# A new program order for the attention stage and the first weight conversions, with the engine of each PSUM copy chosen anew

## The chip, the cores and the metric

The kernel runs on one core of a Trainium2 chip as one program. The metric is the device time of that program in microseconds (us). The median of three runs of the kernel before is 977.77 us (975.89 to 978.73). The profile is one further execution: it took 975.42 us, of which the trace covers a span of 973.6 us.

A core has five engines, each with its own instruction queue that runs strictly in order: TensorE (PE for its matmuls, PEld for its weight loads), VectorE (DVE), ScalarE (ACT), GpSimd (POOL) and SyncE (SP), which here issues nearly all DMAs. They wait for one another by semaphores only. TensorE writes to PSUM, and what it writes has to be copied out by VectorE or ScalarE.

## What is computed

Three layers follow one another:

```python
# 4 x 8 heads, 576 positions, 64 dimensions: rotary attention
q_rot, k_rot = rotate(q), rotate(k)
scores = matmul(q_rot, k_rot.T) / sqrt(D)
attn = exp(scores - max(scores)); attn /= sum(attn) + 1e-9
x = matmul(attn, v)                      # 2304 tokens x 512
# dense layer, 512 -> 2048 -> 512
h = maximum(x @ w_in, 0); x = (h * h) @ w_out
# one of 8 experts per token, 512 -> 1024 -> 512, scaled by the gate
out[mask] = gate[mask] * (maximum(x[mask] @ w1[e], 0) @ w2[e])
```

## The kernel before, in words

Attention is cut into 16 problems, numbered p = 0 to 15, each of two heads. The work on one problem is a set of named steps. These are the names that the texts use:

- `ldq`, `ldk`, `ldv` load q, k, v by DMA; there is one buffer each for raw q and raw k. `aq bq cq` and `ak bk ck` are the rotary products and their sum (128x576 each, lines 189 to 194).
- `qh`, `kh` round q and k to the fast matmul type (line 198). `ql`, `kl0`, `kl1` take the rest that rounding left (lines 205, 208). `qd0` to `qd2` and `kd0` to `kd2` move halves between partitions (line 212), by DMA or by an engine.
- `sc0` to `sc8` are nine score tiles (line 233): four matmuls of 288 columns each, ten for `sc8`. They go into **two** PSUM buffers in turn. `mx` takes the row maximum of a score tile on VectorE (line 248), `ex` the exponential with its row sum on ScalarE (line 258). Only when `ex` has read a score buffer may TensorE write into it again, so a score tile waits for the exponential of the tile two places earlier in TensorE's order.
- `trm..`, `trrk`, `trrq`, `trrr` transpose the exponentials on TensorE (line 291): four matmuls each, one for `trrr`. `evm..`, `evrk`, `evrq`, `evrr`, `sev` copy the results out of PSUM (lines 308, 274). `pv0`, `pv1` multiply by v, 20 matmuls each (line 323), and `u0`, `u1` copy that out. Transposes and products share four PSUM buffers.
- `sa`, `srec` prepare the reciprocal of the row sums, `rst` stores them. `xr` stores the result; for the first 512 tokens `rld`, `xn`, `xh`, `xl`, `xst` divide and split it at once.

The dense layer needs its weights rounded to the reference's type and split in two parts. Weight piece i goes through `wd` (DMA), `wx` (two ScalarE instructions, lines 474 and 475), `wy` (two on VectorE, lines 479 and 480), `wz` (GpSimd, line 484), `wb` (VectorE, line 490), `wh` (ScalarE, line 504) and `wl` (VectorE or GpSimd, line 507). Two pieces make one of 16 weight chunks. The pieces 0 to 11, up to `wb10`, `wh9` and `wl9`, are steps of the written order; the rest is converted inside the loop of the dense layer, `Weights.slot`. `m10`, `m11`, `m12` are the first-layer matmuls of chunks 0 to 2 of the first 512 tokens, with `re`, `sq` (ScalarE) and `gg`, `gl` (VectorE) after each; `m20` is the second-layer product of chunk 0, which reads `sq0` and `gl0`.

The order is written out by hand. A table gives each step a number and an engine (`D` SP's DMA queue, `T` TensorE, `V` VectorE, `A` ScalarE, `P` GpSimd): `FIRST` for problem 0, `SECOND` for 1, `THIRD` for 2 and 3, `PLAN` for 4 to 15, `TAIL` for the weights and the start of the dense layer. The number plus 18 times p is a sorting key, no more. Line 403 sorts all steps by it and emits them, so the key sets the place in the queue of the step's engine; the semaphores set the time.

```python
        plan = [(t + p * PERIOD, p, name, eng) for p in range(NP)
                for name, (t, eng) in (FIRST, SECOND, THIRD, THIRD, PLAN)[min(p, 4)].items()
...
        for t, p, name, eng in sorted(plan, key=lambda z: z[0]):
```

Of the kernel before, what the change touches and what calls it, by code (L numbers as in the profile page):

```python
# [21 lines left out]
B, H, S, D = 4, 8, 576, 64  # L22
# [12 lines left out]
def f32(ap):  # L35
# [23 lines left out]
}  # L59
FIRST = {  # L60
# [20 lines left out]
}  # L81
SECOND = {
# [19 lines left out]
}  # L102
THIRD = {
# [1129 lines left out]
```

## Time and profile before

| what | value |
|---|---|
| median of three runs | 977.77 us |
| profiled execution, and its span | 975.42 us, 973.6 us |
| TensorE busy, VectorE busy | 908.2 us (93%), 615.4 us (63%) |
| ScalarE busy, GpSimd busy | 468.8 us (48%), 323.1 us (33%) |
| first score matmul | 20.23 us |
| first matmul of the dense layer | 326.43 us |

The time divides at 326.43 us: attention ahead of it, with weight conversions in between, and behind it the dense layer and the experts. Matmuls are pipelined and the end of each is modelled, so the busy time of TensorE counts latencies too: gaps between its weight loads say more. From about 410 us on TensorE's matmuls stand without gaps up to about 900 us.

### The profile page before, as it was taken

To read this page: it belongs to the slowest core of one execution; us is meant where nothing else is said; L and a number is where in the kernel's file an instruction comes from. 1 tells how busy PE (TensorE), PEld (TensorE's weight loads), DVE (VectorE), ACT (ScalarE), POOL (GpSimd) and SP (SyncE) were. 2 spreads that over 40 slices of the span, in tenths; PEclk is the share of its full clock that TensorE was granted. 3 is DMA by queue.
4 is the path that set the end of the run, shared out by engine and by line. 5 is a ranking of instruction groups with operands and counts; after the bars stand their busy time and mean duration, and the time that the engine had idled before them with its cause. 6 is when DMAs were issued, how large, how long until landed. Compare 5 with 4: busy or idle time off the path is not lost. (4 is left out here: it accounts for less than half of the span.)

```text
span 973.6 us, 14639 instructions
## 1 busy us (share of the span) xinstructions
PE 908.2 (93%) x5210; PEld 748.4 (77%) x5210; DVE 615.4 (63%) x1120; ACT 468.8 (48%) x946; POOL 323.1 (33%) x258
## 2 busy tenths in 40 slices
PE   1889899989989999999999999999999999999996
PEld 0767667767767676788888888888988889999995
DVE  5776666776766799947554654665373856666650
ACT  3666666666666777542223223222333345555551
POOL 6776775675673366601001100100010123112011
PEclk9999999999999999999999999999999999999998
DMA  7566556546644556451003001100141268777630
GB/s 244 154 177 186 151 132 167 154 119 170 200 122 128 172 169 204 127 165 53 1 1 120 11 1 60 28 1 1 44 173 66 87 182 263 233 223 242 203 107 34
DMA packets 51233, 123.48 MB, mean 127 GB/s; under 512 B 11072, under 2 KB 15184, under 8 KB 51152
## 3 DMA queue, kind: packets, MB, share of 16 engines
q1 hardware_dynamic: 48112, 112.76, 38.6%
q0 software_dynamic: 3040, 9.70, 2.8%
q8 instruction: 43, 0.70, 0.3%
q14 instruction: 38, 0.31, 0.1%
HBM read 93.45 MB, written 15.54 MB: 112 GB/s over the span
## 5 line engine op out<-in xcount | busy, mean ns | idle before, releaser
L250 DVE TENSOR_REDUCE nmx<-sc 128x1 f32<-128x576 f32 x144 | 106.8, 750 | 81.1 <-PE sc L245 80.9
L650 PE MATMUL h<-xs,w 128*128 128x512 f32 (+1 forms) x660 | 145.6, 369 | 4.8 <-DVE w L507 4.6
L656 ACT ACTIVATE r<-h 128x512 f32<-128x512 f32 (+1 forms) x80 | 44.2, 553 | 215.1 <-PE h L650 202.6
L245 PE MATMUL sc<-kh,q 128*128 128x288 f32 (+2 forms) x336 | 102.8, 340 | 46.1 <-ACT e L261 25.2
L261 ACT ACTIVATE e<-sc,nmx 128x576 f32<-128x576 f32 x144 | 106.3, 741 | 76.4 <-DVE nmx L250 76.0
L650 PEld LDWEIGHTS h<-xs,w 128*128 128x128 f32 x660 | 115.1, 188 | 30.0 <-DVE w L507 7.6
L664 DVE SCALAR_TENSOR_TENSOR h<-h,r 128x512 f32<-128x512 f32 (+1 forms) x80 | 51.5, 644 | 124.5 <-ACT r L656 124.3
L684 PE MATMUL y<-w,gh 128*128 128x512 f32 x396 | 122.7, 391 | 0.0
L245 PEld LDWEIGHTS sc<-kh,q 128*128 128x128 f32 x336 | 62.9, 196 | 74.3 <-ACT e L261 44.9
L922 DVE TENSOR_TENSOR w<-eraw,w 128x1024 fp32r<-128x1024 f32 x64 | 78.4, 1226 | 33.5 <-ACT w L921 33.4
L245 PE MATMUL sc<-kl,q 128*128 128x288 f32 (+2 forms) x336 | 91.5, 306 | 0.0
L303 PE MATMUL b<-ident,e 128*128 128x128 f32 x640 | 86.0, 274 | 2.4 <-ACT e L261 2.0
L684 PEld LDWEIGHTS y<-w,gh 128*128 128x128 f32 x396 | 73.3, 188 | 14.5
L571 POOL TENSOR_TENSOR xraw<-xraw,rbs 128x512 f32<-128x512 f32 (+1 forms) x14 | 16.6, 1191 | 197.0 <-DMA rbs<-rD 193.5
L684 PE MATMUL y<-w,gl 128*128 128x512 f32 x198 | 77.1, 389 | 0.0
L968 PEld LDWEIGHTS h<-ye,w 128*128 128x128 f32 x576 | 74.0, 189 | 3.7
L303 PEld LDWEIGHTS b<-ident,e 128*128 128x128 f32 x640 | 73.6, 141 | 3.8 <-ACT e L261 2.9
L968 PE MATMUL h<-ye,w 128*128 128x256 f32 x576 | 74.8, 280 | 0.0
L991 PE MATMUL y<-w,ge 128*128 128x512 f32 x288 | 74.6, 394 | 0.0
L332 PE MATMUL b<-et,v 128*64 128x288 f32 x512 | 73.0, 425 | 0.1
L921 ACT ACTIVATE w<-eraw 128x1024 fp32r<-128x1024 f32 x64 | 67.3, 1052 | 4.1 <-DMA eraw<-wexp 4.1
L998 POOL DMA_INDIRECT out<-ob,six x19 | 22.2, 1169 | 140.1 <-ACT ob L997 107.8
(213 smaller groups left out, 1701.4 us busy)
## 6 DMA issues: line engine op xcount, KB each, us to landing
eraw<-wexp SPq DMA_DIRECT2D x64, 512.0 KB
wraw<-wio SPq DMA_DIRECT2D x32, 512.0 KB
rawq<-qx SPq DMA_DIRECT2D x15, 576.0 KB
rawk<-kx SPq DMA_DIRECT2D x15, 576.0 KB
kh<-kh SPq DMA_DIRECT2D x45, 144.0 KB
v<-v SPq DMA_DIRECT2D x16, 320.0 KB
q<-ql SPq DMA_DIRECT2D x32, 144.0 KB
yD<-ysb SPq DMA_DIRECT2D x18, 256.0 KB
```

What stands on the lines that cost most here:

```text
L245: nc.tensor.matmul(out=o[:, x:x + w], lhsT=q[:, hd, q0:q0 + 128], rhs=k[:, hd, y:y + w], start=(n == 0), stop=(n == len(ops) - 1))
L250: nc.vector.tensor_reduce(out=m, in_=sc(p, j)[:, :, 0:HS], axis=AX.XY, op=ALU.max, negate=True)
L261: nc.scalar.activation(out=e(p)[:, o:o + S].rearrange("p (a b) -> p a b", a=2), in_=sc(p, j)[:, :, 0:HS], func=ACTF.Exp, bias=live[p, f"nm ...
L303: nc.tensor.transpose(t[:, i * 128:(i + 1) * 128], x[:, o:o + 128], ident)
L332: nc.tensor.matmul(out=o[64 * hd:64 * hd + 64], lhsT=lhsT, rhs=rhs, start=(c == 0), stop=(c == 4))
L650: nc.tensor.matmul(out=h, lhsT=w[:, a, k * 128:(k + 1) * 128], rhs=xs[b, k][:, c], start=(k == 0 and i == 0), stop=(k == 3 and i == 2))
L664: nc.vector.scalar_tensor_tensor(out=h, in0=h, scalar=W_SC, in1=rs[n], op0=ALU.mult, op1=ALU.mult)
L684: nc.tensor.matmul(out=yp[t], lhsT=g[a][:, t * 128:(t + 1) * 128], rhs=w[:, c, 512:1024], start=(f == 0 and i == 0), stop=(f == NFC - 1 an ...
L921: nc.scalar.activation(out=w[:, 0], in_=r, func=ACTF.Copy)
L922: nc.vector.tensor_tensor(out=w[:, 1], in0=r, in1=f32(w[:, 0]), op=ALU.subtract)
L968: nc.tensor.matmul(out=h, lhsT=w[:, a, k * 128:(k + 1) * 128], rhs=x[:, c], start=(k == 0 and i == 0), stop=(k == 3 and i == 2))
L991: nc.tensor.matmul(out=yp[s, t], lhsT=g[a][:, t * 128:(t + 1) * 128], rhs=w[:, c, 512:1024], start=(f == 0 and i == 0), stop=(f == EFC - 1 ...
```

## The change

Only the numbers and engine letters of the five tables change. No step is added or removed, and no function changes; two lines of `PLAN` and one of `TAIL` stand here for all.

```diff
-    "ak": (-98.423, "P"), "ck": (-97.690, "P"), "kh": (-97.204, "A"), "cq": (-96.360, "P"), "qh": (-94.409, "V"),
-    "kd0": (-94.211, "D"), "ql": (-93.978, "V"), "kd1": (-93.003, "D"), "kl0": (-92.725, "P"), "qd0": (-92.656, "D"),
...
+    "qh": (-102.8623, "A"), "ql": (-102.7975, "P"), "ldk": (-101.9928, "D"), "ak": (-100.9528, "P"),
...
-    "wx4": (-254.209, "A"), "wy3": (-251.056, "V"), "wb2": (-215.057, "V"), "wz3": (-210.181, "P"),
...
+    "wx4": (-286.6154, "A"), "wy4": (-275.3811, "V"),
```

In `PLAN`, `qh` goes from VectorE to ScalarE, `ql` from VectorE to GpSimd, and `kl1` from GpSimd to VectorE; of the copies, `evm02`, `evm03`, `evm11`, `evrq`, `evrr` and `u1` go from ScalarE to VectorE and `evm00`, `evm01`, `evm12`, `evrk` and `u0` the other way; `evm10`, `sev` and `evm13` stay. In `FIRST` all three `qd` and `kd` moves are made by engines and none by DMA, and k is rotated ahead of q. Of the loaded pieces of the weights, 6 to 10 are converted earlier.

On TensorE, in the written order of problems 9 and 10, this stood between the end of one score tile (`sc2`, here sc_2194) and the start of the one that takes its PSUM buffer (`sc4`, here sc_2223); sc_2208 is `sc0`, and the row with ident is one transpose step of four matmuls.

```order
L245 MATMUL sc_2194<-kl0_87,q0_83 128x288
L303 MATMUL b_2203<-ident_63,e1_90 128x128 x4
L245 MATMUL sc_2208<-kh0_85,q0_83 128x288
L245 MATMUL sc_2208<-kl0_87,q0_83 128x288
L245 MATMUL sc_2208<-kh0_85,q0_83 128x288
L245 MATMUL sc_2208<-kl0_87,q0_83 128x288
L245 MATMUL sc_2223<-kh0_85,q0_83 128x288
```

In the changed kernel the same three tiles are sc_2193, sc_2234 and sc_2251, and this stands between them on TensorE (L303 is `trrr`).

```order
L254 MATMUL sc_2193<-kl0_87,q0_83 128x288
L312 MATMUL b_2201<-ident_63,e1_90 128x128 x4
L312 MATMUL b_2208<-ident_63,e1_90 128x128 x4
L312 MATMUL b_2213<-ident_63,e1_90 128x128 x4
L312 MATMUL b_2218<-ident_63,e1_90 128x128 x4
L254 MATMUL sc_2234<-kh0_85,q0_83 128x288
L254 MATMUL sc_2234<-kl0_87,q0_83 128x288
L254 MATMUL sc_2234<-kh0_85,q0_83 128x288
L254 MATMUL sc_2234<-kl0_87,q0_83 128x288
L303 MATMUL b_2241<-ident_63,e1_90 128x128
L254 MATMUL sc_2251<-kh0_85,q0_83 128x288
```

Three more transpose steps and `trrr` have moved in between the two tiles that share a buffer; the pair of tiles after them was spread in the same way.

On ScalarE, in the same place, these rows stood from the exponential of `sc1` (sc_2163) to that of `sc2` (sc_2194): the row sums `rs`, two pieces of `rk` and one copy `et1`.

```order
L261 ACTIVATE e0_89<-sc_2163,nmx_2183 128x576
L176 ACTIVATE rs_2199<-b_2185 9x128
L176 ACTIVATE rk1_92<-b_2185 64x64 x2
L176 ACTIVATE et1_2170<-b_2188 128x512
L261 ACTIVATE e0_89<-sc_2194,nmx_2215 128x576
```

In the changed kernel (problems 11 and 12 here, whose rows are alike) the two exponentials stand next to each other, with copies ahead of them and behind them.

```order
L185 ACTIVATE et0_2555<-b_2600 128x512
L270 ACTIVATE e0_89<-sc_2583,nmx_2612 128x576
L270 ACTIVATE e0_89<-sc_2606,nmx_2637 128x576
L185 ACTIVATE et1_2576<-b_2621 128x512
L185 ACTIVATE et1_2576<-b_2626 128x512
```

The copies that stood between the two exponentials are gone from there. At the start of the dense layer VectorE had these rows from `gg0` (h_3491) to `gg1`, with weight conversions (L479 to L507) between them.

```order
L664 SCALAR_TENSOR_TENSOR h_3491<-h_3491,r_3517 128x512
L668 TENSOR_TENSOR gl_3522<-h_3491,gh_3519 128x512
L507 TENSOR_TENSOR wf_3478<-wmag_3458,wf_3478 128x512
L490 SCALAR_TENSOR_TENSOR wmag_3480<-wraw_3256,wmag_3480 128x512
L664 SCALAR_TENSOR_TENSOR h_3504<-h_3504,r_3542 128x512
```

In the changed kernel chunk 1 comes first (h_3510), then chunk 0 (h_3534, whose `gl0` is gl_3579) and chunk 2 (h_3559).

```order
L673 SCALAR_TENSOR_TENSOR h_3510<-h_3510,r_3523 128x512
L488 TENSOR_SCALAR wmag_3528<-wmag_3528 128x512
L489 TENSOR_SCALAR wmag_3528<-wmag_3528 128x512
L677 TENSOR_TENSOR gl_3554<-h_3510,gh_3552 128x512
L673 SCALAR_TENSOR_TENSOR h_3534<-h_3534,r_3557 128x512
L516 TENSOR_TENSOR we_3459<-wmag_3292,we_3459 128x512
L673 SCALAR_TENSOR_TENSOR h_3559<-h_3559,r_3574 128x512
L677 TENSOR_TENSOR gl_3579<-h_3534,gh_3572 128x512
L677 TENSOR_TENSOR gl_3584<-h_3559,gh_3582 128x512
```

`gl0` now stands behind `gg2`, which waits for the matmuls of chunk 2, and fewer conversions stand among these rows.

## Rows read from the trace of the kernel before

**Rows 1.** The page: the span.

```profile
span 973.6 us, 14639 instructions
```

**Rows 2.** Stretches: us, then busy per engine (instructions), granted clock, DMA share, GB/s.

```profile
20.20:96.84 76.64, 65.90 (x444) 52.51 (x444) 52.86 (x73) 47.76 (x117) 56.23 (x43) 0.98 0.63 176
96.84:318.68 221.84, 204.23 (x1474) 155.39 (x1473) 152.37 (x225) 142.29 (x356) 139.33 (x109) 0.98 0.54 150
209.89:228.02 18.13, 16.78 (x125) 12.86 (x124) 12.38 (x19) 11.57 (x30) 11.40 (x9) 1.00 0.55 156
340.00:405.00 65.00, 60.41 (x256) 47.02 (x255) 62.95 (x94) 46.25 (x81) 44.03 (x31) 1.00 0.56 181
```

**Rows 3.** Waits, 96.8 to 318.7 us: total us, times, longest.

```profile
PEld sc L245 <- ACT e L261: 32.3, 67, 1.6
```

**Rows 4.** Waits, 20.2 to 96.8 us.

```profile
PEld sc L245 <- ACT e L261: 12.6, 15, 2.0
```

**Rows 5.** Timeline, weight loads of one problem: start, us, what, [idle before, releaser].

```profile
211.72 0.19 PEld L245 LDWEIGHTS sc<-kh,q 128*128 128x128 f32 x1 [0.15 <-ACT e L261]
...
212.27 0.45 PEld L303 LDWEIGHTS b<-ident,e 128*128 128x128 f32 x4
...
212.99 0.19 PEld L245 LDWEIGHTS sc<-kh,q 128*128 128x128 f32 x1 [0.27 <-ACT e L261]
...
215.10 0.19 PEld L245 LDWEIGHTS sc<-kh,q 128*128 128x128 f32 x1 [1.55 <-ACT e L261]
...
215.82 0.19 PEld L245 LDWEIGHTS sc<-kh,q 128*128 128x128 f32 x1 [0.16 <-ACT e L261]
...
216.54 1.65 PEld L332 LDWEIGHTS b<-et,v 128*64 128x64 f32 x16 [0.16 <-issue]
...
219.12 0.19 PEld L245 LDWEIGHTS sc<-kh,q 128*128 128x128 f32 x1 [0.44 <-issue]
```

**Rows 6.** Timeline, VectorE and ScalarE in the same problem.

```profile
210.05 0.75 DVE L250 TENSOR_REDUCE nmx<-sc 128x1 f32<-128x576 f32 x1
...
210.84 0.74 ACT L261 ACTIVATE e<-sc,nmx 128x576 f32<-128x576 f32 x1 [0.54 <-DVE nmx L250]
...
212.56 0.76 DVE L250 TENSOR_REDUCE nmx<-sc 128x1 f32<-128x576 f32 x1 [0.42 <-PE sc L245]
...
213.73 0.60 ACT L176 ACTIVATE et<-b 128x512 f32<-128x512 f32 x1
...
214.22 0.73 ACT L261 ACTIVATE e<-sc,nmx 128x576 f32<-128x576 f32 x1
```

**Rows 7.** Groups by line and shape: busy us, mean ns, idle before.

```profile
L178 DVE CAST q<-rawq 128x576 fp32r<-128x576 f32 x15 | 24.3, 1620 | 10.6 <-POOL rawq L194 10.6
...
L176 ACT ACTIVATE q<-rawq 128x576 fp32r<-128x576 f32 x1 | 0.7, 666 | 0.0
```

**Rows 8.** Line 181 on VectorE: ns min/median/max, first and last start.

```profile
L181 DVE TENSOR_TENSOR ql<-rawq,q x16: 748/758/1965, 13.2 to 291.5; 128x576 fp32r<-128x576 f32 x16
```

**Rows 9.** Timeline, the preparation of k and q: issues of SP, work of GpSimd.

```profile
199.32 1.11 SPq L220 DMA_DIRECT2D kh<-kh  x1
...
201.45 1.42 POOL L181 TENSOR_TENSOR kl<-rawk,kh 64x576 fp32r<-64x576 f32 x1 [0.96 <-DMA kh<-kh]
...
201.66 0.33 SPq L187 DMA_DIRECT2D rawq<-qx  x1
...
206.21 1.43 POOL L192 TENSOR_TENSOR rawq<-rawq,tabq 128x576 f32<-128x576 f32 x1 [3.35 <-DMA rawq<-qx]
```

**Rows 10.** Timeline, the start: ScalarE's first weight piece and the first score matmul.

```profile
11.95 0.64 ACT L475 ACTIVATE wraw<-wraw 128x512 f32<-128x512 uint32 x1
...
20.23 0.58 PE L245 MATMUL sc<-kh,q 128*128 128x288 f32 x1 [20.23 <-ACT kh L176]
```

**Rows 11.** Waits, 326 to 410 us.

```profile
PEld h L650 <- DVE w L507: 7.6, 8, 1.0
```

203 rows, old and new, of tables (FIRST, PLAN, SECOND, TAIL) are left out of this document.

## The prediction

> **What bounds the kernel now.** I read the stretches first [rows 2]. TensorE is the engine with the most busy time in attention, 16.78 of 18.13 us for one problem, against 12.38 on VectorE, 11.57 on ScalarE and 11.40 on GpSimd. From 340 to 405 us it is VectorE, 62.95 of 65. So in attention the question is what TensorE waits for. The list of waits has one answer: the exponentials on ScalarE, which free the score buffers, 32.3 us in 67 waits from problem 4 on and 12.6 us in the first four [rows 3, 4]. The timeline of one problem shows where [rows 5]: 0.15, 0.27, 1.55 and 0.16 us ahead of four score tiles, 2.13 us in all. The gaps of 0.16 and 0.44 around the product with v wait for no other engine ("issue"). I count them as TensorE's own; some of the 32.3 us are such gaps under another name.
>
> Why is one wait 1.55 us? Rows 6 show a tile that is served at once and one that isn't. Served at once: maximum from 210.05, exponential from 210.84, weight load of the next tile at 211.72 [rows 5, 6], so 1.67 us from the start of the maximum. A maximum starts 0.29 us after the tile's last issue (212.27 to 212.56). A score buffer is therefore away for at least 1.96 us, and TensorE needs that much other work between two tiles of one buffer. Ahead of `sc4` it has one score tile (211.72 to 212.27, 0.55) and one transpose step (0.45), 1.0 us. Besides, ScalarE makes a 0.60 us copy at 213.73 and smaller ones before it, while the maximum has been ready since 213.32: the exponential starts at 214.22, 0.9 us late.
>
> **The change, part by part.** It removes and adds no instruction; it moves them.
>
> *Problems 4 to 15.* In the new order I add up, with the same prices, TensorE's work between two tiles of one buffer. One score tile is 0.55, one transpose step 0.45, `sc8` 10/4 of a score tile or 1.4, a product with v with its gaps 2.6 (216.54 to 219.12). Ahead of `sc3` of the next problem stand `sc8` and two steps, 2.3; of `sc1` two steps, one tile, two steps, 2.35; of `sc2` the same; of `sc0` six steps and a tile, 3.25; of `sc4` four steps, a tile and `trrr`, 2.4 at least; of `sc6`, `sc5`, `sc7` and `sc8` a product and a tile, 3.15 each. None is under 1.96. Then the engines have to serve at once. On ScalarE a single copy (`evm01`, 0.60) may stand ahead of `ex1`, and `sc0`, which waits for that, has 3.25; `ex2` follows directly. `qh` stands ahead of `ex8`: there the maximum of the long `sc8` isn't ready any earlier. VectorE has at most one large copy, of about that size, between two maxima. So the 2.13 us per problem should go but for a few hundredths: I take 2.1 x 12 = 25.2 us. What is late next is TensorE itself, at 18.13 - 2.13 = 16.0 us per problem. Bounds: 0, if the waits only move, and 32.3, all of rows 3.
>
> What must stay hidden for this: `qh` costs VectorE 1.62 and ScalarE 0.67 [rows 7]. ScalarE with 11.57 of 18.13 has room for it and VectorE is relieved. `ql` on GpSimd, at the price of the other GpSimd pieces (1.42), replaces `kl1` there, so its 11.40 per problem stay and fit into 16.0. The earlier weight pieces stand in the gaps that VectorE keeps between `sc4` and `sc6`, where TensorE makes 2.6 us of product; without that cover each would cost about such a copy, 0.6 us, once.
>
> *Problems 0 to 3.* The same rule, but rotation is shared with VectorE and the interleaving is different in each, and `pv0` and `pv1` come one problem later, which leaves TensorE something to do while it waits. I take half of the waits on exponentials, 6 us. Bounds: 3 lost to 12.6 gained [rows 4].
>
> *The start.* ScalarE's first weight piece ends at 12.59, the first score is at 20.23 [rows 10]. In the new order k is rotated first, and behind that weight piece ScalarE has `kh`, `kd0`, `kd1`, `qh`, `qd0`, two instructions of a weight piece, `kd2`, `qd1`: nine at about 0.66 [rows 7, 10], 5.9 us, to 18.5. That is 1.7 us gained; bounds 0 and 2.5. DMAs no longer make q's moves there, so `ldq` of problem 1 is freed earlier, too.
>
> *The dense layer.* TensorE waits eight times 0.95 us for converted weights, while VectorE is full [rows 2, 11]. With fewer conversions left behind attention VectorE comes in ahead, and the lead is used up over the ten chunks: I take half, 3.8 us. On the other side `gl0` now stands behind `gg2`. `m20` reads `gl0` after two matmuls, and nothing but it is queued on TensorE: from the end of `m12` it waits for `re2`, `gg2` and `gl0`, three instructions of 128x512. At the 0.60 of such a copy [rows 6] I estimate 1.8 us lost. Together 2.0 gained; bounds 1.8 lost and 7.6 gained.
>
> *Sum.* 25.2 + 6 + 1.7 + 2.0 = 34.9 us off the profiled execution of 975.42 (span 973.6 [rows 1], 1.8 around it): 940.5. The median of the runs stands 2.35 above that execution, so 943 us.
>
> **A rule that speaks against it.** VectorE's two-input subtraction takes 0.758 us in the median and up to 1.965 [rows 8]; `kl1` is now one of these, beside GpSimd's rotation. The Trainium skill, in "SBUF — State Buffer", section "Who interferes with whom", says that a VectorE instruction with two SBUF inputs shares a port pair with a GpSimd instruction that reads SBUF, and whichever comes second waits for all of the other. By it `kl1` would take 0.76 and up to 1.4 more in each problem and push the next maximum by some 0.3 us; the sum would be 12 x 0.3 = 4 us higher, 947. The median of rows 8 doesn't show it, the maximum may.
>
> **The rivals.**
> 1. *The waits move only in part.* Copies are shared out anew, and the product with v needs the last of them; if half of the 2.13 us comes back there or at a maximum, the problems give 12.8 instead of 25.2, the first four 3: 19.5 off, 958 us. For it: both engines stand within a few tenths of being late for `sc3` and `sc4`. Against: rows 5 show each wait with a cause that the new order takes away.
> 2. *Attention becomes faster than I say.* All of rows 3 and 4 that isn't "issue" goes and the weight waits vanish: 27 + 12.6 + 1.7 + 5.8 = 47 off, 931 us. For it: nothing in the sums above forbids it. Against: the first problems also wait for their own k and q.
> 3. *Slower: the single buffer of raw k becomes the loop.* `ldk` now waits for `kl1`, which stands on VectorE behind the last maxima. A load of 576 KB takes 4.55 us from issue to the first use (201.66 to 206.21 [rows 9]); then `ql`, `ak`, `bk`, `ck` on GpSimd, 4 x 1.42 = 5.7; `kh` 0.7; the move 2.1 (199.32 to 201.45); `kl1` 0.8: 13.9 us, under 16.0. With waits for a place in each queue it decides from 2.1 us more on. At 16.0 all is as forecast; to eat up the other 9.7 us of gain too it has to reach 18.13 + 0.8 = 18.9. At 19.5 the kernel takes 12 x 1.37 = 16.4 more and 9.7 less: 984 us. For it: GpSimd waits 3.35 us for such a load already, and it is in order, so `sa` and `kl0` are queued behind. Against: 2.1 us of room, and the DMA share of 0.55 is far from full.
> 4. *It doesn't do what it says:* the loop is held at 18.1 by something that no view shows, and only start and dense layer count: 3.7 off plus 0 to 6, 971 us.
>
> **How the numbers follow.** Likeliest: 943, itself 934 to 951, chance 0.66. Rival 1 has 0.14, rival 2 0.11, rival 3 0.05, rival 4 0.04. The range for 8 in 10 reaches half into rival 2 and over rival 1: 929 to 962. A measurement of this kernel can tell some 0.3%, 3 us, from no change: slower by more than that is rival 3 (0.05), within it the edge of rival 4 (0.02), the rest is faster (0.93).
>
> **What would show it.** Right: the steps `srec` of neighbouring problems 16.0 to 16.3 us apart from problem 6 on; no weight load of a score tile with a wait on `e` above 0.4; first score near 18.5; attention's last product near 293; in the dense layer four weight waits of 0.9 at most, not eight, and one of 1.8 at the first L693. Wrong: distances of 17 or more, with GpSimd waiting for raw k (rival 3) or the first `pv0` matmul for a copy (rival 1); a first score after 20; a granted clock under 1.00 in most problems would mean that something else has changed.

## The result, and the profile after

The changed kernel takes 945.12 us (median of 4 runs, 944.62 to 947.58), the kernel before 976.85 us in the same series (4 runs). The ratio is 0.9678, with a 95% interval of 0.9654 to 0.9702. Forecast were 943 us and a range of 929 to 962. In the changed file every line stands nine further down: L245 is now L254, L261 L270, L332 L341, L650 L659, L684 L693.

| moment in the profile | before | after |
|---|---|---|
| first score matmul | 20.23 | 19.58 |
| `srec` of problem 3 | 97.67 | 94.03 |
| `srec` of problem 15 | 318.95 | 287.15 |
| first matmul of the dense layer | 326.43 | 295.96 |
| span | 973.6 | 942.7 |

Of 30.9 us, 28.2 come between the `srec` of problems 3 and 15, 3.6 ahead of that. 1.3 are lost at the end of attention (7.48 us before, 8.81 now) and 0.4 come behind it. The stretches, as in [rows 2]:

```profile
19.58:94.03 74.45, 63.71 (x431) 54.62 (x431) 61.19 (x85) 54.53 (x129) 54.94 (x41) 0.93 0.55 161
94.03:287.15 193.12, 188.14 (x1481) 151.03 (x1480) 166.22 (x259) 145.44 (x340) 142.40 (x108) 1.00 0.64 182
192.89:208.44 15.55, 15.55 (x125) 12.72 (x124) 12.21 (x21) 11.98 (x28) 11.86 (x10) 1.00 0.63 175
```

In the third row TensorE's busy time is the whole stretch: a problem without a wait takes 15.55 us, where it took 18.13. Its weight loads show why; nothing but the gaps around the product with v is left of [rows 5]:

```profile
194.11 0.19 PEld L254 LDWEIGHTS sc<-kh,q 128*128 128x128 f32 x1
...
194.84 1.65 PEld L341 LDWEIGHTS b<-et,v 128*64 128x64 f32 x16 [0.16 <-ACT et L185]
...
197.41 0.19 PEld L254 LDWEIGHTS sc<-kh,q 128*128 128x128 f32 x1 [0.44 <-ACT e L270]
```

The waits on exponentials, from problem 4 on and in the first four, answer to [rows 3, 4], which had 32.3 and 12.6 us:

```profile
PEld sc L254 <- ACT e L270: 9.1, 13, 2.4
...
PEld sc L254 <- ACT e L270: 10.9, 13, 2.5
```

They aren't gone. 9.1 us in 13 waits are left in the steady problems, the longest of 2.4 us, where the forecast's sign of being right was none above 0.4. The steps of `srec` (us from one problem to the next, problem 1 first) show where:

| kernel | steps |
|---|---|
| before | 18.68 21.33 19.93, 19.73 19.21 18.13 18.13 19.72 18.13 18.12 18.13 18.15 18.12 18.13 17.58 |
| changed | 20.64 16.63 18.58, 13.63 20.33 17.04 15.60 16.71 15.55 15.55 16.22 15.59 17.76 15.58 13.56 |

Take the problem of 17.76. VectorE makes `kl1` and then one piece of the weights in two instructions, all from SBUF to SBUF, and each takes over 1.5 us. The maximum behind them is late, and so is the exponential for which TensorE waits:

```profile
247.12 1.80 DVE L190 TENSOR_TENSOR kl<-rawk,kh 64x576 fp32r<-64x576 f32 x1
248.95 1.54 DVE L488 TENSOR_SCALAR wmag<-wmag 128x512 f32<-128x512 f32 x1
250.52 1.52 DVE L489 TENSOR_SCALAR wmag<-wmag 128x512 int32<-128x512 int32 x1
251.96 0.75 DVE L259 TENSOR_REDUCE nmx<-sc 128x1 f32<-128x576 f32 x1
...
253.62 0.19 PEld L254 LDWEIGHTS sc<-kh,q 128*128 128x128 f32 x1 [2.37 <-ACT e L270]
```

The step to problem 3 (18.58) has the same pattern: the first `kl1` of `PLAN` stands behind a weight piece there, and the transposes wait for the exponential.

```profile
79.41 1.67 DVE L488 TENSOR_SCALAR wmag<-wmag 128x512 f32<-128x512 f32 x1
81.11 1.53 DVE L489 TENSOR_SCALAR wmag<-wmag 128x512 int32<-128x512 int32 x1
82.68 1.72 DVE L190 TENSOR_TENSOR kl<-rawk,kh 64x576 fp32r<-64x576 f32 x1
...
86.10 0.29 PEld L312 LDWEIGHTS b<-ident,e 128*128 128x128 f32 x2 [2.54 <-ACT e L270]
```

All pieces of `kl` on VectorE together (min/median/max in ns) answer to [rows 8]: a median of 1.6 us, where the shortest takes 0.74.

```profile
L190 DVE TENSOR_TENSOR kl<-rawk,kh x13: 743/1605/1875, 16.9 to 265.0; 64x576 fp32r<-64x576 f32 x13
```

The start and the dense layer: the first weight piece on ScalarE (in [rows 10] its second instruction began at 11.95) and the first score; the weight waits, eight and 7.6 us in [rows 11]; and `m20`, which waits for `gl0`.

```profile
12.29 0.65 ACT L483 ACTIVATE wmag<-wraw 128x512 f32<-128x512 f32 x1 [10.27 <-DMA wraw<-wio]
...
19.58 0.58 PE L254 MATMUL sc<-kh,q 128*128 128x288 f32 x1 [19.58 <-ACT q L185]
...
PEld h L659 <- DVE w L516: 3.7, 4, 1.0
PEld y L693 <- DVE gl L677: 2.0, 1, 2.0
...
307.14 0.50 PE L693 MATMUL y<-wf,gl 128*128 128x512 f32 x1 [1.56 <-DVE gl L677]
```

**The granted clock** moves sums of this size, so it has to be read before any of them. In the kernel before two neighbouring steps, the same work, stood at different clocks:

```profile
154.74:172.87 18.13, 16.79 (x126) 12.88 (x125) 12.38 (x20) 11.58 (x29) 11.57 (x10) 1.00 0.59 141
172.87:192.59 19.72, 18.36 (x126) 13.62 (x124) 13.05 (x20) 11.69 (x29) 12.63 (x11) 0.91 0.58 153
```

A mean of 0.91 is a part of the step at 1.2 GHz, the rest at 2.4; it cost 1.6 us. The profiles have such dips in different places. Before had three in attention, one of them ahead of the `srec` of problem 3; the changed kernel has three, all ahead of that, at 0.91 (ahead of the `srec` of problem 0), 0.90 and 0.91. The last two:

```profile
58.82:75.45 16.63, 15.31 (x111) 14.43 (x113) 12.91 (x21) 13.52 (x35) 13.83 (x11) 0.90 0.53 155
75.45:94.03 18.58, 16.27 (x119) 13.54 (x115) 14.73 (x21) 12.05 (x31) 13.44 (x12) 0.91 0.60 172
```

The first can't be set against the kernel before. The clock view shows nothing ahead of the first rise, but the same weight load takes 0.33 us at the start and 0.19 later (and 0.33 again inside the dips), so TensorE began at 1.2 GHz: in the kernel before until some 31 us, in the changed kernel until some 24.

```profile
30.87 0.33 PEld L245 LDWEIGHTS sc<-kl,q 128*128 128x128 f32 x1
31.63 0.19 PEld L245 LDWEIGHTS sc<-kl,q 128*128 128x128 f32 x1
...
23.83 0.33 PEld L254 LDWEIGHTS sc<-kl,q 128*128 128x128 f32 x1
25.00 0.19 PEld L254 LDWEIGHTS sc<-kl,q 128*128 128x128 f32 x1
```

(The first two rows are of the kernel before, the others of the changed one.) How much of problem 0 this cost isn't known. In a second profile of the changed kernel (`changed_again` below) the loads took 0.33 until 34.6 us, and the `srec` of problem 0 came only 0.34 us later than here.

The changed kernel has another dip in the dense and expert stage: TensorE waits 2.28 us for gathered rows until 693.14, and the stretch around the end of that wait has

```profile
692.00:696.00 4.00, 2.83 (x9) 2.43 (x10) 1.27 (x3) 1.35 (x3) 1.32 (x2) 0.67 0.88 320
696.00:700.00 4.00, 4.00 (x26) 3.59 (x25) 2.41 (x4) 1.44 (x4) 0.00 (x0) 0.91 0.33 96
```

That is 0.33 x 4 + 0.09 x 4 = 1.7 us lost. In the profile of before a wait of 2.05 us stood at the same place (so its matmuls don't stand quite without gaps there), and the clock stayed at 1.00. One more dip comes later in each of the two profiles (at 779 and 748 us), and these cancel.

### The profile page after: what moved, and what is told of

Same layout as the page of the kernel before. It is cut to its first block, busy times and chain, and to the rows that moved or that the text cites. A ratio compares the mean times of both kernels' runs of the same rounds, so it can differ in the third digit from the quotient of the medians.

```text
span 942.7 us, 14580 instructions
## 1 busy us (share of the span) xinstructions
PE 890.3 (94%) x5210; PEld 748.5 (79%) x5210; DVE 625.8 (66%) x1151; ACT 473.0 (50%) x929; POOL 320.7 (34%) x251
## 5 line engine op out<-in xcount | busy, mean ns | idle before, releaser
L659 PE MATMUL h<-xs,w 128*128 128x512 f32 (+1 forms) x660 | 145.1, 369 | 2.3 <-DVE w L516 2.0
L659 PEld LDWEIGHTS h<-xs,w 128*128 128x128 f32 x660 | 115.8, 188 | 25.7 <-DVE w L516 3.7
L270 ACT ACTIVATE e<-sc,nmx 128x576 f32<-128x576 f32 x144 | 106.3, 740 | 52.9 <-DVE nmx L259 51.9
L254 PE MATMUL sc<-kh,q 128*128 128x288 f32 (+1 forms) x336 | 98.4, 330 | 31.4 <-ACT q L185 19.6
L693 PE MATMUL y<-w,gh 128*128 128x512 f32 x396 | 123.6, 393 | 0.0
L254 PEld LDWEIGHTS sc<-kh,q 128*128 128x128 f32 x336 | 63.0, 196 | 47.3 <-issue 22.6
L254 PE MATMUL sc<-kl,q 128*128 128x288 f32 (+1 forms) x336 | 90.3, 304 | 0.0
L312 PE MATMUL b<-ident,e 128*128 128x128 f32 x640 | 84.1, 278 | 3.9 <-ACT e L270 3.3
L693 PEld LDWEIGHTS y<-w,gh 128*128 128x128 f32 x396 | 73.8, 189 | 14.6
L693 PE MATMUL y<-w,gl 128*128 128x512 f32 x198 | 77.6, 392 | 0.0
L341 PE MATMUL b<-et,v 128*64 128x288 f32 x512 | 70.0, 412 | 1.0 <-DVE et L187 0.8
```

The source lines that it names most:

```text
L254: nc.tensor.matmul(out=o[:, x:x + w], lhsT=q[:, hd, q0:q0 + 128], rhs=k[:, hd, y:y + w], start=(n == 0), stop=(n == len(ops) - 1))
L270: nc.scalar.activation(out=e(p)[:, o:o + S].rearrange("p (a b) -> p a b", a=2), in_=sc(p, j)[:, :, 0:HS], func=ACTF.Exp, bias=live[p, f"nm ...
L312: nc.tensor.transpose(t[:, i * 128:(i + 1) * 128], x[:, o:o + 128], ident)
L341: nc.tensor.matmul(out=o[64 * hd:64 * hd + 64], lhsT=lhsT, rhs=rhs, start=(c == 0), stop=(c == 4))
L659: nc.tensor.matmul(out=h, lhsT=w[:, a, k * 128:(k + 1) * 128], rhs=xs[b, k][:, c], start=(k == 0 and i == 0), stop=(k == 3 and i == 2))
L693: nc.tensor.matmul(out=yp[t], lhsT=g[a][:, t * 128:(t + 1) * 128], rhs=w[:, c, 512:1024], start=(f == 0 and i == 0), stop=(f == NFC - 1 an ...
```

## The experiments

Each was timed in five rounds beside the kernel before; the ratio is to that kernel, with its 95% interval.

**1 and 2. The parts of the change.** `plan_only` is the kernel before with the new PLAN alone, `rest_only` the changed kernel with the old PLAN.

```diff
 (plan_only)  PLAN: all numbers and letters new; FIRST, SECOND, THIRD, TAIL old
 (rest_only)  PLAN old; FIRST, SECOND, THIRD, TAIL new
```

> Of the five tables only PLAN (problems 4 to 15) is the new one. Theory: the waits for the exponentials sat in the steady problems, whose steps came 18.44 us apart on average before and 16.09 after; 12 x 2.35 = 28.2 less 1.3 for a longer end of attention is 27 us, so 950 us (946 to 955), with problems 15.6 us apart wherever no weight piece is in the way. Rival: the gain needs all tables fitted to each other, because PLAN's tail of one problem is interleaved with the head of the next and the weight pieces stand where the old order left room; then at most half of it comes, 962 us or more.

> PLAN is the old one; FIRST, SECOND, THIRD and TAIL are new. Theory: only the first four problems (3.6 us by the steps of problem 3 in the two traces) and the dense layer (3.8 us of weight waits gained, 1.6 lost at the first product with the second weights) remain: 5 to 6 us off, 971 us (967 to 976), problems still 18.1 us apart. Rival: the earlier weight pieces and the new head do a good part of it also in the steady state; then 962 or less, with problems nearer 17.

Measured: `plan_only` 964.68 us, 0.9889 (0.9864 to 0.9913); `rest_only` 985.04 us, 1.009 (1.0065 to 1.0115), slower. Alone they give 11 off and 9 more, together 32 off, so the parts don't add up. But the steady state is PLAN's: in `plan_only` the steps from problem 5 on are 15.47 15.74 15.58 16.21 16.77 15.61 16.56 17.33 15.58 15.48 13.20, in `rest_only` 18.1 to 19.8 (the 19.75 with a dip of the clock, 0.91). What is lost is lost at the seams of the tables, in SP's queue. In `plan_only` the last load of v stands in it behind three loads of the dense layer's input that still wait; TensorE then waits for v:

```profile
293.78 7.50 SPq L539 DMA_DIRECT2D xs<-xT  x3
301.33 0.59 SPq L230 DMA_DIRECT2D v<-v  x1
...
307.25 4.11 PE L334 MATMUL b<-et,v 128*64 128x288 f32 x16 [7.23 <-DMA v<-v]
```

In `rest_only` SP issues nothing from 107.6 to 124.86, until a load of v; the store of `xh` is behind that, and ScalarE, in order too, stands for 12 us with exponentials behind it. The step from problem 4 to 5 is 32.04.

```profile
106.38 1.23 SPq L294 DMA_DIRECT2D rb<-rD  x2
124.86 0.33 SPq L236 DMA_DIRECT2D v<-v  x1
125.29 0.57 SPq L369 DMA_DIRECT2D xT<-xh  x1
...
129.71 0.63 ACT L184 ACTIVATE xh<-xo 128x512 fp32r<-128x512 f32 x1 [12.18 <-DMA xT<-xh]
```

So both my theories on the size of a part fall, since I had priced no seam; the rival that the tables are fitted to each other holds, though not its reason for the steady state.

**3 and 4. Order and engines in PLAN.** Both start from the kernel before.

```diff
-    "qh": (-94.409, "V")
+    "qh": (-102.8623, "V")      order_only: new numbers, old letters, all of PLAN
+    "qh": (-94.409, "A")        letters_only: old numbers, new letters
```

> In the kernel before, PLAN gets the new numbers but keeps the old engine letters. Theory: the order is the cause, above all the work of TensorE between two score tiles of one buffer and the exponentials next to each other; it brings two thirds or more of what the whole new PLAN brings, so 952 to 960 us, and the wait of 1.55 us ahead of the score tile that waited longest is gone. Rival: the choice of engines is the cause (large copies off ScalarE, one engine relieved); then order alone is no better than 968, or slower than before, with waits for copies in the product with v.

> In the kernel before, PLAN keeps the old numbers but gets the new engine letters. Theory: the 1.0 us of TensorE's work between the two tiles stays, so a wait of at least 1.96 - 1.0 = 0.96 us in each problem stays; gain between 0 and 0.6 x 12 = 7 us, 970 to 977 us, or a loss of some us where the copies now collide with maxima. Rival: the engines are the cause; then 960 or less.

Measured: `order_only` 970.53 us, 0.9948 (0.9928 to 0.9967); `letters_only` 997.52 us, 1.0218 (1.0195 to 1.0242). The steady steps are 16.76 and 20.4 us (18.13 before, 15.6 with both). Order alone takes 1.4 us off a problem; on top of the new order the letters give another 1.2. In `order_only` the wait of 1.55 is gone, and what is left is short and mostly for copies:

```profile
209.84 0.42 PEld L305 LDWEIGHTS b<-ident,e 128*128 128x128 f32 x4 [0.34 <-DVE et L180]
...
213.83 0.19 PEld L247 LDWEIGHTS sc<-kh,q 128*128 128x128 f32 x1 [0.49 <-ACT e L263]
```

In `letters_only` it is longer than before; the new copies now stand among the old order's exponentials:

```profile
224.48 0.19 PEld L245 LDWEIGHTS sc<-kh,q 128*128 128x128 f32 x1 [1.93 <-ACT e L261]
```

But most of the 2.3 us that the letters alone add to a problem is the clock. It stays at 1.00 in the step to problem 5, and in each of the ten later ones it is 0.91 or 0.92, with a stretch at 1.2 GHz that begins 0.1 to 0.4 us after the long wait:

```profile
118.42:137.33 18.91, 16.50 (x123) 12.83 (x123) 11.46 (x20) 11.62 (x28) 13.32 (x12) 1.00 0.60 167
157.73:178.21 20.48, 18.05 (x125) 13.72 (x123) 11.59 (x21) 11.54 (x28) 11.66 (x10) 0.92 0.49 132
163.20:166.50 3.30, 3.30 (x15) 2.24 (x16) 1.52 (x2) 2.22 (x6) 1.12 (x2) 0.50 0.23 49
```

By the 1.6 us that a dip cost above, such a step would take some 18.8 us at the full clock, an estimate, so that the letters alone add 0.7 by waits and the rest through the clock.

So the new order is the cause, and the letters pay only with it. Which queue's place in the order does it was not tried apart, but for ScalarE's in the next experiment: that TensorE's is the main part rests on the sums of the prediction and on the waits that went. The total of `order_only` missed its forecast by the seams again (step 2 takes 29.24 us).

**5. ScalarE's copies alone.** Three numbers in the kernel before, so that `ex2` comes ahead of the small copies.

```diff
-    "sev": (-63.680, "A"), "evrr": (-63.483, "A"), "evm10": (-61.985, "A")
+    "sev": (-61.73, "A"), "evrr": (-61.72, "A"), "evm10": (-61.71, "A")
```

> The kernel before with three numbers changed in PLAN: sev, evrr and evm10 (the row sums, the last pieces and one copy on ScalarE) come behind the exponentials ex2 and ex0 instead of ahead of ex2. No engine and nothing of TensorE's order changes. Theory: of the wait of 1.55 us 0.9 is ScalarE's being busy with those, the rest the missing work of TensorE: 0.6 to 0.9 us off each of 12 problems, 966 to 970 us, and a wait of about 0.65 stays. Rival: the copies are now late for the product with v or for the transposes' buffers, and the wait only moves: 974 to 979 us.

Measured: 976.17 us, 0.9988 (0.9971 to 1.0004), no difference; steps of 18.44, at a clock of 1.00 in all of them, against 18.13. The rival holds in the total. The wait for `sc4` falls from 1.55 to 0.68, by 0.87, where the theory gave ScalarE's copies 0.9, and leaves what it gave to the missing work of TensorE (0.65). But the next score tile gets 0.71 and the product with v 0.45 for the copy put off:

```profile
213.03 0.19 PEld L245 LDWEIGHTS sc<-kh,q 128*128 128x128 f32 x1 [0.68 <-ACT e L261]
214.30 0.19 PEld L245 LDWEIGHTS sc<-kh,q 128*128 128x128 f32 x1 [0.71 <-ACT e L261]
...
215.68 1.40 PEld L332 LDWEIGHTS b<-et,v 128*64 128x64 f32 x13 [0.45 <-ACT et L176]
```

That the total is no longer although each steady problem is, goes with the clock: a mean of 0.991 to 0.998 in its runs, 0.984 to 0.993 in those of the kernel before.

**6 to 8. Three edits of the changed kernel**, one at a time: `kl1` back on GpSimd; `gl0` ahead of `gg2`; the first two weight pieces of ScalarE behind the moves of problem 0.

```diff
-    "kl1": (-89.1905, "V")
+    "kl1": (-89.1905, "P")                              kl1_gpsimd
-    "gl0": (876.006, "V")
+    "gl0": (871.3, "V")                                 gl0_first
-    "wx2": (-674.0967, "A"), "wx0": (-619.2397, "A")
+    "wx2": (-614.0, "A"), "wx0": (-613.9, "A")          start_late_w
```

> The changed kernel with kl1 of PLAN back on GpSimd, nothing else. Theory: beside GpSimd kl1 takes up to 1.9 us on VectorE instead of 0.74, and with weight pieces that take 1.5 us there instead of 0.42 it makes the maxima behind it late; in four of the problems TensorE then waits 0.6 to 2.4 us for an exponential, 5.6 us in all. With kl1 away VectorE has 1.3 to 1.9 us more: 3 to 5 us faster than the changed kernel, 941 us, most steps 15.6 us apart. Rival: GpSimd, 13.4 us busy of 15.6, gets 1.4 us more and makes kl late for the next problem's score tiles: same or slower, 945 to 955 us.

> The changed kernel with gl0 ahead of gg2 on VectorE, nothing else. Theory: TensorE's wait of 1.56 us at the first product with the second weights goes, and nothing takes its place, since TensorE is the engine that bounds from there on: 1.5 us faster, 943.6 us. Rival: VectorE is full in that stretch, so the waits for converted weights grow by as much: no difference, 945 us.

> The changed kernel with ScalarE's first two weight pieces (wx2, wx0) put behind the last move of problem 0. Theory: k is rotated by 9.1 us, but ScalarE waits until 12.29 for a weight transfer that stands ahead of kh, and makes a second piece at 16.9; without both kh runs at 9.1, q's half at 12, and the first score tile at about 15 instead of 19.58. TensorE then also starts 4.6 us earlier; with the waits of the first problems I expect 3 to 4.6 us off, 941 us. Rival: problems 1 and 2 are held by their own loads and rotations, which start when raw k and q are free or by bytes, and eat it up: 945 us, with longer waits between 20 and 60 us.

Measured: `kl1_gpsimd` 941.02 us, 0.9635 (0.9613 to 0.9658); `gl0_first` 944.92, 0.9664 (0.9637 to 0.9691); `start_late_w` 942.89, 0.9653 (0.9626 to 0.9679). The changed kernel stands at 0.9678 and, run again below, at 0.9691. So `kl1` is worth 4 to 5.5 us, the total that the theory gave. But it doesn't lie where the theory had it. Most steps are 16.0 to 17.4, not 15.6. Over problems 4 to 15 the four profiles with `kl1` on VectorE have 193.1, 196.3, 197.2 and 197.9 us (the changed kernel, `changed_again`, `gl0_first`, `start_late_w`), the four without it, here and below, 194.5, 194.6, 195.2 and 195.0: 1.3 less on average, within the spread. The rest comes ahead of that, 2.9 to 4.6 us up to the `srec` of problem 3, and most of it in one step, to problem 3, which takes 15.3 instead of 17.3 to 18.8. There the wait of 2.54 us, the same within 0.01 in all four with `kl1` on VectorE, becomes

```profile
82.92 0.20 PEld L313 LDWEIGHTS b<-ident,e 128*128 128x128 f32 x2 [0.65 <-ACT e L271]
```

and the dip of the clock that stands beside that wait in three of those four (0.91) is in none of the four without it. The other two edits are within what these intervals tell. Their traces show that the waits did go: `m20` has none left in `gl0_first`, and the first score comes at 15.7 instead of 19.58 in `start_late_w`, of which 2.4 us are left at the `srec` of problem 0. But other stretches grew. In `gl0_first`, whose order in attention is that of the changed kernel, two steps take 18.1 us instead of 15.60 and 16.71 (17.7 and 18.0 in `start_late_w`):

```profile
148.60 4.43 DVE L490 TENSOR_SCALAR wmag<-wmag 128x512 int32<-128x512 int32 x1
...
148.57 1.42 POOL L191 TENSOR_TENSOR kl<-rawk,kh 64x576 fp32r<-64x576 f32 x1 [0.80 <-ACT kh L186]
149.96 2.79 POOL L202 TENSOR_TENSOR rawq<-rawq,tabq 128x576 f32<-128x576 f32 x2
```

An instruction of 0.43 us took 4.43: it came 0.03 us behind GpSimd's, and lasted until three of GpSimd's were through. In the changed kernel the same one started 0.16 us ahead of GpSimd's, took 0.43, and GpSimd's took 1.54:

```profile
148.62 0.43 DVE L489 TENSOR_SCALAR wmag<-wmag 128x512 int32<-128x512 int32 x1
...
148.78 1.54 POOL L190 TENSOR_TENSOR kl<-rawk,kh 64x576 fp32r<-64x576 f32 x1 [0.80 <-ACT kh L185]
```

**9 to 12. Together, in one series**: the changed kernel again, `kl1` and `gl0`, all three edits, and all three with three weight pieces on VectorE moved.

```diff
-    "wx6": (-161.6278, "A"), "wy6": (-160.1285, "V"), "wy9": (-124.7944, "V"), "wb5": (-215.9663, "V"), "wh5": (-214.5411, "A")
+    "wx6": (-164.0, "A"), "wy6": (-163.5, "V"), "wy9": (-109.5, "V"), "wb5": (-199.5, "V"), "wh5": (-199.0, "A")    three_slots
```

> The changed kernel itself, beside the three that follow. 945 us; the profile tells which of the longer steps between problems come back and which are chance.

> The changed kernel with kl1 of PLAN on GpSimd and gl0 ahead of gg2. Theory: the two gains are in different stretches and add: about 4 us in attention and 1.5 in the dense layer, 939.5 us. Rival: the second wait was covered (weight pieces held VectorE anyway); then 941, as with kl1 alone.

> Besides kl1 and gl0 the first two weight pieces of ScalarE come behind the moves of problem 0. Theory: the step srec of problem 0 is 2.4 us earlier, and with VectorE free of kl1 nothing eats it up later: 2 us less than with the two, 937.5 us. Rival: the pieces put off meet VectorE and GpSimd in problems 1 to 3 and the gain is lost there, no difference.

> As the kernel with the three edits, and three weight pieces on VectorE (the magnitudes of pieces 6 and 9, the blend of piece 5) go from the place ahead of mx7, where GpSimd rotates q beside them, to the place two maxima earlier, where GpSimd waits for k; wx6 and wh5 are moved with them. Theory: VectorE's work between SBUF tiles is stretched only while GpSimd reads SBUF too: at the first place such a piece took 1.5 to 4.4 us, at the second 0.42 each; the waits of 0.8 to 1.6 us for exponentials in those three problems go, 2 to 3 us off. Rival: the length of the pieces has another cause, or GpSimd's work moves along with them; then no difference.

| kernel | us | ratio to before |
|---|---|---|
| `changed_again` | 946.54 | 0.9691 (0.9668 to 0.9713) |
| `kl1_gl0` | 940.10 | 0.9621 (0.9600 to 0.9642) |
| `all_three` | 938.78 | 0.9598 (0.9576 to 0.9620) |
| `three_slots` | 938.74 | 0.9598 (0.9571 to 0.9625) |

`all_three` beats both kernels: 7.8 us less than the changed one in the same series. The two edits of `kl1_gl0` give 6.4 of that; the late weight pieces 1.3, near the 1.7 by which their `srec` of problem 0 is earlier, but not beyond the intervals. In `changed_again` steps of 17.40 and 17.02 stand where 15.60 and 16.71 stood, though the order is the same: how long such a step is differs from run to run. Its 19.29 in place of 17.76 is something else, a dip of the clock (0.91).

`three_slots` is a miss. The magnitudes of piece 6 did come to the earlier place, but there they waited 1.96 us for ScalarE and then ran beside GpSimd's rotation all the same; the exponential is late by 1.94:

```profile
208.53 1.27 DVE L489 TENSOR_SCALAR wmag<-wmag 128x512 f32<-128x512 f32 x1 [1.96 <-ACT wmag L484]
209.83 1.52 DVE L490 TENSOR_SCALAR wmag<-wmag 128x512 int32<-128x512 int32 x1
...
212.99 0.19 PEld L255 LDWEIGHTS sc<-kh,q 128*128 128x128 f32 x1 [1.94 <-ACT e L271]
```

Whether pieces in GpSimd's gaps would pay stays open. What is late next, with `kl1` on GpSimd, is `qh`: in `kl1_gpsimd` it waits on ScalarE 0.88 us for GpSimd's rotation, with an exponential queued behind it for which TensorE then waits 0.79 us (at 234.31).

## Why the prediction was right, point by point

| term | forecast | measured | estimate without the dips of the clock (1.6 each, 1.7 in the dense layer) |
|---|---|---|---|
| problems 4 to 15 | -25.2 | -28.2 | -25.0 (before had two dips, after none) |
| problems 0 to 3 | -6 | -3.0 | -4.6 (behind problem 0: before one, after two) |
| start | -1.7 | -0.65 | -0.65 |
| end of attention | 0 | +1.3 | +1.3 |
| dense layer | -2.0 | -0.4 | -2.1 |
| sum | -34.9 | -30.9 | -31.1 |

- *The steady problems* were the bulk, and the reason was the right one: TensorE's own work now covers a buffer's way through maximum and exponential. `order_only`, in which the wait of 1.55 is gone, and `act_only`, in which 0.68 of it is left where the sums leave 0.65, speak for it. That the sum fits so well is partly luck. A clean problem takes 15.55 us, not the 16.0 of the forecast: TensorE's weight loads stood idle 18.13 - 12.88 = 5.25 us per problem before and 15.55 - 12.72 = 2.83 after, 2.4 us less, where the marked waits that I added up had given 2.13. Against that stand the long steps, 16.2 to 17.8, that I hadn't in the sum. And this profile is the best of four with the same order in attention: without their dips the gain in these problems is 25.0 here and 20.9 to 23.4 in `changed_again`, `gl0_first` and `start_late_w`.
- *Problems 0 to 3*: half of the waits was a guess, and it was too much: 3.0 us came, 4.6 by the estimate. The waits on exponentials fell only from 12.6 to 10.9 us.
- *The step that failed in size* is "VectorE has at most one large copy, of about that size, between two maxima", with 0.6 us for a weight piece without cover. VectorE had a `kl1` of 1.6 us in the median and instructions of a weight piece of 1.5 us there, up to 4.4 in other profiles, and up to three such instructions in a row (1.80, 1.54 and 1.52 us at 247.12). It is the rule that I weighed and left out of the sum: the Trainium skill, "SBUF — State Buffer", section "Who interferes with whom". It says that a VectorE instruction with two SBUF inputs and a GpSimd instruction that reads SBUF exclude each other, the later one blocked for the whole of the other. The trace agrees for `kl1`: 1605 ns in the median against 743 at least. My price for it, 0.3 us in each of twelve problems, is not what the runs show: by the profiles the 4 to 5.5 us of `kl1_gpsimd` are mostly one wait ahead of problem 3 and the clock beside it, and that the total is near my 4 us is luck. The forecast by the rule was 947, without it 943; 945 lies between. An instruction of a weight piece has one SBUF input; the section names `tensor_scalar` among those that can contend too, in a mode with two ports. Taken literally that gives 0.43 + 1.42 = 1.85 us, an estimate; the 4.43 us of `gl0_first` are more, and there the measurement decides.
- *ScalarE's copies*, "0.9 us late", were read rightly: `act_only` takes 0.87 us off that wait by moving them. But that gains nothing, since other waits take its place.
- *The start*: the count of nine instructions was right, its beginning wrong. ScalarE's first weight piece came 0.9 us later than before, at 12.29, and k was ready at 9.1 us; `start_late_w`, without that wait of 3.2 us and without the 2.4 us of the two weight pieces, has the first score at 15.74; which of the two holds it wasn't parted.
- *The end of attention* wasn't in the sum. The last product waits 0.61, 0.82 and 0.17 us for copies, where nothing is interleaved any more.
- *The dense layer*: four weight waits instead of eight, as forecast; `m20` waits 1.56 us, 1.8 were forecast. A dip of the clock ate the rest. That it followed the wait of 2.28 us within 0.2 us is what the rows show; that the wait made it isn't shown.
- *The rivals*: that half the waits only move (1), a loop over raw k (3) and no effect (4) are refuted by the steps of 15.55, and that all waits go (2) by those that are left. The condition of rival 3, GpSimd waiting for raw k in each problem, doesn't appear; from problem 4 on it waits three times:

```profile
POOL rawk L201 <- DMA rawk<-kx: 2.2, 3, 1.0
```

## What to carry to other kernels

In a ring of two buffers, count the bounding engine's own work between two uses of one buffer against the buffer's way through the other engines: where it is less, TensorE waited here whatever ScalarE's order (`act_only`), and where it is more, small delays vanish. An order written out by hand is one piece: half of a new one cost 9 us, because queues in order (SP's above all) were crossed at the seam. And before a term of 2 us is explained, look at the granted clock of its stretch: in `letters_only` most of the difference was there.

## What the runs showed of the hardware that was not expected

- A VectorE instruction between SBUF tiles that takes 0.43 us alone took up to 4.43 us beside GpSimd: its own time and three GpSimd instructions (1.42 and two in 2.79), without a turn in between. A blend of weights took up to 4.65 (0.68 in the median). Which of the two engines waits hung on 0.03 to 0.16 us. Maxima that read PSUM took 0.76 us at most throughout.
- By that, the same order gave steps of 15.60 and 16.71, 17.40 and 17.02, or 18.13 and 18.12 us in the same two problems of three profiles (the changed kernel, `changed_again`, `gl0_first`).
- Each dip of the clock in attention in the profiles of the kernel before, the changed kernel and `letters_only` began within 2 us of the end of a TensorE wait of 1.5 to 2.5 us. In `letters_only` one followed each of ten such waits in a row (1.87 to 2.21 us), in the kernel before only two of the thirteen of 1.5 us behind problem 3. What decides between them isn't shown.
